# Gate sums as contraction rows of the score matmul, one constant causal tile, and unsplit float32 scores for every second head of batch 0

## The chip, the cores and the metric

The kernel runs on one core of one Trainium2 chip. The metric is the device time of one execution in microseconds (us), as the median of several runs. TensorE (PE; its weight loads are PEld) does the matmuls, VectorE (DVE), ScalarE (ACT) and GpSimd (POOL) the elementwise work, and SyncE (SP) issues all DMAs from one queue, in order.

## The reference, cut to what matters

Three stages follow each other on a batch of 4, 8 heads, 576 positions and a head dimension of 64: causal attention with a forget gate, a SwiGLU layer (512 to 1536 to 512), and a SiLU layer (512 to 2048 to 512), the latter two on all 2304 tokens.

```python
scores = scale * np.matmul(q, k.transpose(0, 1, 3, 2))         # scale = 1/8
cum = np.cumsum(np.maximum(s, 0.0), axis=-1)
bias = -(cum[:, :, :, None] - cum[:, :, None, :])
scores = np.where(causal, -1000000000.0, scores + np.minimum(bias, 0.0))
attn = softmax(scores); x = attn @ v                            # then heads side by side
x = (silu(x @ w_gate) * (x @ w_val)) @ w_out
out = silu(x @ w_in) @ w_out2
```

In a row of scores the term of the row's own position is a constant, which softmax removes; what stays is, per key position, the running sum `cum` of that head, and the causal mask.

## The kernel before, in words

**Matmul forms.** Most matmuls are of the type fp32r, which keeps fewer bits than float32, so a float32 operand is split into a high and a low part (hi = rounded copy, lo = operand minus hi). The scores of a head (`a_scores`, line 227) use two matmuls per tile. The 128 contraction rows hold the 64 rows of K rounded (`ks`, upper half) and the remainder of K (lower half); the other side is Q rounded, twice (`qh`), and the remainder of Q, twice (`ql`). `a_split` (line 197) makes these four pieces: a rounding copy of K on ACT (line 207), one of Q on DVE or ACT by the batch (208), the subtraction for K's lower half (210, on DVE in batch 0 and on POOL later), the subtraction for Q (212, on POOL in batch 0 and on DVE later). The attention output of batch 0 (`a_pv`, `WHOLE_P`) is computed from unsplit float32 operands; such a matmul stands in the trace as two instructions.

**Gate and mask.** `setup` (128) computes `cum` for all 32 heads on DVE. Each head's row must stand on all 128 partitions (`cumb`): for the first two heads by a matmul with a picked column of the identity and two ACT copies (lines 183 to 187), for the others by a DMA that repeats the row of 576 numbers 128 times (189, 288 KB). For every score tile POOL makes a masked copy of the part of `cumb` that holds the diagonal (line 235), and one DVE instruction adds scores and gate and takes the row's minimum of the negated sum (line 250). Where the masked part does not begin at the tile's left edge this takes two such instructions.

**After the scores.** ACT takes the exponential with its row sum (260), DVE makes the reciprocal (269, 270), POOL scales the row (117, called at 274), PE transposes it (292), ACT and DVE move the transposes out of PSUM, and PE multiplies by V (328).

**Staging.** A head is done in two halves: A holds the query tiles of 64, 128 and 128 rows, B two of 128. Each of the 64 half heads is a slot. Slot u emits the scores of unit u, the split of the next head and the loads of the head after it (with half A), the product with V of unit u-2 and the transposes of unit u-1 (`slot_pieces`, 548). The 18 first slots (all of batch 0) stand ahead of the feed-forward stream; the weights of its first two chunks are loaded and decoded from slot 8 on. After that, each chunk of the first layer carries two slots of the next batch between its steps. The weights come as 8 bytes per number on first use, are decoded by ACT and DVE (413 to 420), written back as float32 to DRAM (423) and read again in later batches; ACT, POOL and DVE split them (433, 434). The second layer follows with no attention left.

**What sets the order.** Instructions are emitted in the order of `body` (575), and a planner places them on each engine by emission order among those that its own timing has ready. On the chip each engine then runs its list in order. Pools limit how far ahead things go: two buffers of `qkr` (Q and K as loaded), `cumb`, `ks`, `qh`, `ql`, V; six of the score rows `e`, where `cum` and the setup's scratch tiles live at first.

Of the kernel before, what the change touches and what calls it, by code (L numbers as in the profile page):

```python
# [17 lines left out]
P = 128  # L18
# [49 lines left out]
def kernel(  # L68
# [98 lines left out]
    def a_load(b, h, halves):  # L167
        k1, v1, q0 = SPAN[halves]
        t = qkr_p.tile([P, 2, S], F32, tag="qkr", name="qkr")
        rows = (0,) if (b, h) in WHOLE_S else (0, D)  # L170
        if q0 == 0:
            src = qk[b, h, :, :, :k1].rearrange("t d s -> d t s")
            for lo in rows:
                nc.sync.dma_start(out=t[lo : lo + D, :, :k1], in_=src)
        else:
            for lo in rows:
                nc.sync.dma_start(out=t[lo : lo + D, 0, q0:k1], in_=qk[b, h, 0, :, q0:k1])
                nc.sync.dma_start(out=t[lo : lo + D, 1, :k1], in_=qk[b, h, 1, :, :k1])
        c = cum_p.tile([P, S], F32, tag="cumb", name="cumb")
        hh = b * H + h  # L180
        if hh < 2:
            for n0, n in ((0, min(k1, 320)), (320, k1 - 320)):
                if n > 0:
                    ps = ps_a.tile([P, 512], F32, tag="a", name="pcb")
                    pick = ident[: B * H, hh : hh + 1].to_broadcast([B * H, P])
                    nc.tensor.matmul(out=ps[:, :n], lhsT=pick, rhs=cum[:, n0 : n0 + n], start=True, stop=True)
                    nc.scalar.activation(out=c[:, n0 : n0 + n], in_=ps[:, :n], func=AF.Copy)
        else:
# [5 lines left out]
        st[b, h, halves] = (t, c, xa, xb)  # L194
        loads.append(last)

    def a_split(b, h, halves):
        k1, v1, q0 = SPAN[halves]
        t, c, xa, xb = st.pop((b, h, halves))
        if (b, h) in WHOLE_S:  # L200
            ks, qs = t[:D, 1], (t[:D, 0],)
        else:
            ks = qks_p.tile([P, S], F32R, tag="ks", name="ks")
            qh = qks_p.tile([P, S], F32R, tag="qh", name="qh")
            ql = qks_p.tile([P, S], F32R, tag="ql", name="ql")
            qs = (qh, ql)
# [3 lines left out]
            eng.tensor_tensor(out=ks[D:P, :k1], in0=t[D:P, 1, :k1], in1=ks[D:P, :k1].bitcast(F32), op=ALU.subtract)  # L210
            eng = nc.gpsimd if b in POOL_QL else nc.vector
            eng.tensor_tensor(out=ql[:, q0:k1], in0=t[:, 0, q0:k1], in1=qh[:, q0:k1].bitcast(F32), op=ALU.subtract)
        if (b, h) not in WHOLE_P:
            va_s = first_v[(b * H + h) % 3]
            vb_s = v_p.tile([P, 4, 2, D], F32R, tag="vsb", name="vsb")
            copy(VHI[b], va_s[:D, 0, :], xa)
            copy(VHI[b], vb_s[:, :v1, 0, :], xb[:, :v1])
            nc.vector.tensor_tensor(out=va_s[:D, 1, :], in0=xa, in1=va_s[:D, 0, :].bitcast(F32), op=ALU.subtract)
            eng = nc.gpsimd if b in POOL_V else nc.vector
            eng.tensor_tensor(  # L220
                out=vb_s[:, :v1, 1, :], in0=xb[:, :v1], in1=vb_s[:, :v1, 0, :].bitcast(F32), op=ALU.subtract
            )
            xa, xb = va_s.rearrange("p t d -> p (t d)"), vb_s.rearrange("p j t d -> p j (t d)")
        for half in halves:
            st[b, h, half, "in"] = (ks, qs, c, xa, xb)

    def a_scores(b, h, half, i):
        ks, qs, c, _, _ = st[b, h, half, "in"]
        q0, r = TILES[i]
        wd = q0 + r  # L230
        e = e_p.tile([P, S], F32, tag="e", name="e")

        g0 = 0 if wd <= 320 else 320
        nc.gpsimd.affine_select(
            out=e[:r, g0:wd], in_=c[:r, g0:wd], pattern=[[-1, wd - g0]], compare_op=ALU.is_ge,
            fill=-8.0 * QMASK, base=q0 - g0, channel_multiplier=1,
        )
        m = None
        for c0, n in ((0, wd),) if wd <= 512 else ((0, g0), (g0, wd - g0)):
            ps = ps_a.tile([P, 512], F32, tag="a", name="psc")  # L240
            for part, q in enumerate(qs):
                nc.tensor.matmul(
                    out=ps[:, :n], lhsT=q[:, q0 : q0 + P], rhs=ks[:, c0 : c0 + n],
                    start=(part == 0), stop=(part == len(qs) - 1),
                )
            for g, end, gate in ((c0, min(g0, c0 + n), c), (max(g0, c0), c0 + n, e)):
                if g >= end:
                    continue
                m2 = sm_p.tile([P, 1], F32, tag="m", name="m")
                nc.vector.tensor_tensor_reduce(  # L250
                    out=e[:r, g:end], in0=ps[:r, g - c0 : end - c0], in1=gate[:r, g:end], scale=-0.125,
                    scalar=3.0e38 if m is None else m[:r], op0=ALU.add, op1=ALU.min, accum_out=m2[:r],
                )
                m = m2
# [424 lines left out]
```

## Time and profile before

| | us |
|---|---|
| median of 3 runs | 1103.63 |
| lowest, highest | 1102.15, 1104.18 |
| profiled execution, first to last instruction (its span) | 1102.4 |
| PE busy in it | 1073.2 |
| DVE, ACT, POOL busy | 705.1, 587.2, 532.7 |

The profiled execution shows no time of its own beside its span; its span lies between the lowest and the highest of the timed runs. The page's PE share is an upper reading, since matmuls are pipelined and their ends are modelled; how far apart matmuls start is the better one. The profile's rows are given further down.

### The profile page before, as it was taken

How to read it: one execution, taken by the hardware profiler on the slowest of the kernel's cores; microseconds unless marked ns; L12 is line 12 of the kernel's file. 1: busy time of each engine (PE TensorE's matmuls, PEld its weight loads, DVE VectorE, ACT ScalarE, POOL GpSimd, SP SyncE). 2: the span in 40 equal slices, each digit the busy share in tenths (PEclk: the TensorE clock that was granted, in tenths of full speed). 3: DMA queues.
4: the chain of work that ended last, by engine and by line, in shares of the span. 5: the costliest groups of instructions: out<-in, count | busy, mean ns of one | idle time of the engine just before them, and what ended most of it. 6: DMA issues, size and time to landing. Idle time of an engine off the chain costs nothing. (4 is left out here: it accounts for less than half of the span.)

```text
span 1102.4 us, 19356 instructions
## 1 busy us (share of the span) xinstructions
PE 1073.2 (97%) x6760; PEld 994.2 (90%) x6760; DVE 705.1 (64%) x1625; ACT 587.2 (53%) x1294; POOL 532.7 (48%) x611
## 2 busy tenths in 40 slices
PE   7979899999999999999999999999999999999998
PEld 4647899999999999999999999888989898888887
DVE  6877788897778886868765346715364645644333
ACT  4887788875766564666645434655243433422221
POOL 7666677675666664757434453232323222332221
PEclk9988999999999999999999999999999999999999
DMA  5587487785353534533144223711010101000012
GB/s 135 137 242 239 157 216 239 210 250 174 86 143 90 140 95 140 149 83 101 39 154 147 77 86 123 226 41 59 20 58 20 58 20 58 20 1 1 1 61 111
DMA packets 53728, 121.39 MB, mean 110 GB/s; under 512 B 8256, under 2 KB 21568, under 8 KB 53632
## 3 DMA queue, kind: packets, MB, share of 16 engines
q1 hardware_dynamic: 53632, 120.17, 36.8%
q8 instruction: 53, 0.87, 0.3%
q14 instruction: 43, 0.35, 0.1%
HBM read 101.20 MB, written 18.95 MB: 109 GB/s over the span
## 5 line engine op out<-in xcount | busy, mean ns | idle before, releaser
L460 POOL TENSOR_TENSOR h<-u,h 128x288 fp32r<-128x288 f32 (+2 forms) x176 | 193.2, 1099 | 349.5 <-ACT h L113 344.7
L445 PE MATMUL po<-h,wh 128*128 128x288 f32 (+2 forms) x704 | 232.8, 332 | 2.1 <-ACT h L113 1.2
L446 PE MATMUL po<-h,wh 128*128 128x288 f32 (+2 forms) x704 | 232.9, 331 | 0.1
L445 PE MATMUL pgv<-xt,wh 128*128 128x288 f32 x768 | 230.9, 301 | 1.4 <-DVE u L458 0.8
L447 PE MATMUL po<-h,wl 128*128 128x288 f32 (+2 forms) x704 | 232.0, 330 | 0.0
L446 PE MATMUL pgv<-xt,wh 128*128 128x288 f32 x768 | 228.8, 298 | 1.5 <-DVE xt L349 1.5
L447 PE MATMUL pgv<-xt,wl 128*128 128x288 f32 x768 | 228.6, 298 | 0.0
L434 POOL TENSOR_TENSOR wl<-wraw,wh 128x1024 fp32r<-128x1024 f32 x53 | 129.2, 2437 | 113.8 <-ACT wh L113 101.5
L113 ACT ACTIVATE h<-u 128x288 fp32r<-128x288 f32 (+2 forms) x176 | 89.4, 508 | 118.0 <-DVE u L458 66.4
L445 PEld LDWEIGHTS pgv<-xt,wh 128*128 128x128 f32 x768 | 144.9, 189 | 3.0 <-DVE u L458 1.1
L446 PEld LDWEIGHTS pgv<-xt,wh 128*128 128x128 f32 x768 | 145.2, 189 | 2.0 <-DVE xt L349 1.8
L447 PEld LDWEIGHTS pgv<-xt,wl 128*128 128x128 f32 x768 | 145.1, 189 | 0.3
L445 PEld LDWEIGHTS po<-h,wh 128*128 128x128 f32 x704 | 132.0, 188 | 10.2 <-ACT h L113 1.8
L456 DVE SCALAR_TENSOR_TENSOR u<-th,pu 128x464 f32<-128x464 f32 (+1 forms) x80 | 50.7, 633 | 137.9 <-ACT th L454 137.9
L447 PEld LDWEIGHTS po<-h,wl 128*128 128x128 f32 x704 | 132.2, 188 | 7.0
L446 PEld LDWEIGHTS po<-h,wh 128*128 128x128 f32 x704 | 132.2, 188 | 6.9 <-POOL h L460 0.5
L540 DVE SCALAR_TENSOR_TENSOR acc<-po,acc 128x464 f32<-128x464 f32 (+1 forms) x140 | 88.5, 636 | 62.6 <-PE po L447 61.9
L454 ACT ACTIVATE th<-pu 128x464 f32<-128x464 f32 (+1 forms) x80 | 44.1, 552 | 152.2 <-PE pu L447 152.2
L113 ACT ACTIVATE wh<-wraw 128x1024 fp32r<-128x1024 f32 x88 | 92.2, 1056 | 52.0 <-PE po L446 27.1
L446 PE MATMUL pu<-x,wh 128*128 128x464 f32 (+1 forms) x320 | 118.9, 371 | 0.0
L445 PE MATMUL pu<-x,wh 128*128 128x464 f32 (+1 forms) x320 | 118.6, 371 | 0.0
L447 PE MATMUL pu<-x,wl 128*128 128x464 f32 (+1 forms) x320 | 118.5, 370 | 0.0
(87 smaller groups left out, 2012.9 us busy)
## 6 DMA issues: line engine op xcount, KB each, us to landing
wraw<-w SPq DMA_DIRECT2D x54, 512.0 KB, 4.8
r<-in_w_dram SPq DMA_DIRECT2D x52, 512.0 KB, 5.0
qkr<-in_qk_dram SPq DMA_DIRECT2D x64, 288.0 KB, 5.1
w<-wraw SPq DMA_DIRECT2D x18, 512.0 KB, 4.4
cumb<-cum_d SPq DMA_DIRECT2D x30, 288.0 KB, 4.1
r<-in_w_dram SPq DMA_DIRECT2D x32, 256.0 KB, 3.1
x_d<-acc SPq DMA_DIRECT2D x32, 144.0 KB, 3.8
vrb<-in_vb_dram SPq DMA_DIRECT2D x32, 128.0 KB, 4.6
```

Of the source, the lines that this page charges most:

```text
L113: nc.scalar.activation(out=out, in_=in_, func=AF.Copy, scale=scale)
L434: engines[eng].tensor_tensor(out=wl, in0=t, in1=wh.bitcast(F32), op=ALU.subtract)
L445: nc.tensor.matmul(out=ps[:, :n], lhsT=a, rhs=xh, start=(k == 0), stop=False)
L446: nc.tensor.matmul(out=ps[:, :n], lhsT=a, rhs=xl, start=False, stop=False)
L447: nc.tensor.matmul(out=ps[:, :n], lhsT=c, rhs=xh, start=False, stop=(k == last))
L454: nc.scalar.activation(out=th[:, :n], in_=pg[:, :n], func=AF.Tanh, scale=0.5)
L456: nc.vector.scalar_tensor_tensor(out=u, in0=th[:, :n], scalar=1.0, in1=pg[:, :n], op0=ALU.add, op1=ALU.mult)
L460: engines[LO[ph]].tensor_tensor(out=lo, in0=u, in1=hi.bitcast(F32), op=ALU.subtract)
L540: nc.vector.scalar_tensor_tensor(out=a, in0=ps[:, :n], scalar=0.5, in1=a, op0=ALU.mult, op1=ALU.add)
```

## The change

Per head, the gate is no longer added on DVE from a tile of 128 equal rows. It enters the score matmul as contraction rows: against rows of ones on Q's side stand the high and the low part of the head's `cum` row on K's side. Split heads (28 of 32) now use the pairs (`qa`,`ka`) and (`qb`,`kb`): `ka` is K rounded, twice; `qa` is Q rounded in the upper half and Q's remainder in the lower; `kb` holds the remainder of K in 64 rows, two gate rows, and zeros; `qb` holds Q rounded again, two rows of ones, and zeros. `kb` and `qb` are two fixed pairs of tiles whose zeros and ones are written once on POOL. The two gate rows come by a DMA from a DRAM table `cum_d` that now holds high part, low part and whole of every row. The mask is one constant tile `gate_c`, of which every score tile reads a shifted window, so each score tile takes one DVE instruction per PSUM bank. Heads 0, 2, 4 and 6 of batch 0 are not split: their scores are one float32 matmul per bank over 65 rows (64 of Q and K, one of ones and `cum`), straight from the loaded tile.

```diff
-WHOLE_S = []
+WHOLE_S = [(0, h) for h in (0, 2, 4, 6)]
+QUP = "gagg"
-    cum_p = pool("cum", 2, scope=attention, side="right")
+    row_p = pool("row", 1, scope=attention, side="right")
-    cum_d = dram.tile([B * H, S], F32, name="cum_d")
+    chl = [e_p.tile([B * H, S], F32, tag="e", name="chl") for _ in range(2)]
+    cum_d = dram.tile([B * H, 3, S], F32, name="cum_d")
+    gate_c = row_p.tile([P, 448 + P], F32, name="gate")
 def setup():
-        nc.sync.dma_start(out=cum_d, in_=cum)
+        nc.scalar.activation(out=chl[0].bitcast(F32R), in_=cum, func=AF.Copy)
+        nc.vector.tensor_tensor(out=chl[1].bitcast(F32R), in0=cum, in1=chl[0], op=ALU.subtract)
 def zeros():
         nc.gpsimd.memset(z[D:P], 0.0)
+        for n in range(2):
+            kb = row_p.tile([P, S], F32R, tag=f"kb{n}", name="kb")
+            qb = row_p.tile([P, S], F32R, tag=f"qb{n}", name="qb")
+            copy("g", kb[D:P], z[D:P])
+            copy("g", qb[D:P], z[D:P])
+            nc.gpsimd.tensor_scalar(out=qb[D : D + 2], in0=z[D : D + 2], scalar1=1.0, ...)
+            kq_b.append((kb, qb))
+        nc.gpsimd.memset(gate_c, 0.0)
+        nc.gpsimd.affine_select(out=gate_c[:, 448:], ..., fill=-8.0 * QMASK, base=0, channel_multiplier=1)
 def a_load(b, h, halves):
-        rows = (0,) if (b, h) in WHOLE_S else (0, D)
-        ...
-        c = cum_p.tile([P, S], F32, tag="cumb", name="cumb")
-        if hh < 2:
-            ...                     (a matmul with a picked identity column, two ACT copies)
-        else:
-            nc.sync.dma_start(out=c[:, :k1], in_=cum_d[hh : hh + 1, :k1].to_broadcast([P, k1]))
+        for lo in (0,) if whole else (0, D):
+            nc.sync.dma_start(out=t[lo : lo + D], in_=src)
+        if whole:
+            nc.gpsimd.memset(t[D : D + 1, 0], 1.0)
+            nc.sync.dma_start(out=t[D : D + 1, 1], in_=cum[hh : hh + 1] if hh == 0 else cum_d[hh : hh + 1, 2])
 def a_split(b, h, halves):
-            copy(KHI[b], ks[:, :k1], t[:, 1, :k1])
-            copy(QHI[b], qh[:, q0:k1], t[:, 0, q0:k1])
-            eng.tensor_tensor(out=ks[D:P, :k1], in0=t[D:P, 1, :k1], in1=ks[D:P, :k1]..., op=ALU.subtract)
-            eng.tensor_tensor(out=ql[:, q0:k1], in0=t[:, 0, q0:k1], in1=qh[:, q0:k1]..., op=ALU.subtract)
+            nc.sync.dma_start(out=kb[D : D + 2].bitcast(F32), in_=cum_d[hh, :2])
+            copy(KHI[b], ka, t[:, 1])
+            copy(QHI[b], qa, t[:, 0])
+            copy(QUP[b], qb[:D], t[:D, 0])
+            eng.tensor_tensor(out=kb[:D], in0=t[:D, 1], in1=ka[:D].bitcast(F32), op=ALU.subtract)
+            eng.tensor_tensor(out=qa[D:P], in0=t[D:P, 0], in1=qa[D:P].bitcast(F32), op=ALU.subtract)
+            parts = ((qa, ka), (qb, kb))     # unsplit: parts = ((t[: D + 1, 0], t[: D + 1, 1]),)
 def a_scores(b, h, half, i):
-        nc.gpsimd.affine_select(out=e[:r, g0:wd], in_=c[:r, g0:wd], ..., fill=-8.0 * QMASK, ...)
...
-            for g, end, gate in ((c0, min(g0, c0 + n), c), (max(g0, c0), c0 + n, e)):
-                nc.vector.tensor_tensor_reduce(out=e[:r, g:end], in0=ps[...], in1=gate[:r, g:end], ...)
+            g0 = 448 - q0 + c0
+            nc.vector.tensor_tensor_reduce(out=e[:r, c0 : c0 + n], in0=ps[:r, :n], in1=gate_c[:r, g0 : g0 + n], ...)
 def body():
         a_load(*spans[0])
+        for i, x in enumerate((*chl, cum)):
+            nc.sync.dma_start(out=cum_d[:, i], in_=x)
```

## Rows read from the trace of the kernel before

**Rows 1.** The profile's page: the span, and busy us (share) xinstructions of each engine.
```profile
span 1102.4 us, 19356 instructions
...
PE 1073.2 (97%) x6760; PEld 994.2 (90%) x6760; DVE 705.1 (64%) x1625; ACT 587.2 (53%) x1294; POOL 532.7 (48%) x611
```

**Rows 2.** Four stretches: length, busy us per engine, granted clock, DMA share, GB/s.
```profile
28.30:44.90 16.60, 15.89 (x89) 10.24 (x88) 13.23 (x48) 13.35 (x38) 11.59 (x23) 1.00 0.53 137
60.00:90.00 30.00, 24.06 (x107) 14.54 (x106) 21.07 (x64) 25.72 (x64) 19.94 (x32) 0.83 0.93 272
90.00:140.00 50.00, 45.52 (x313) 42.73 (x312) 41.30 (x110) 37.48 (x87) 31.02 (x44) 0.93 0.62 192
200.00:700.00 500.00, 497.81 (x3780) 491.31 (x3779) 356.66 (x883) 294.18 (x678) 282.40 (x317) 1.00 0.44 129
```

**Rows 3.** Timeline of PE within one head of batch 0: start, duration, instruction.
```profile
32.03 0.45 PE L242 MATMUL psc<-ks,qh 128*128 128x448 f32 x1
...
33.36 0.64 PE L328 MATMUL pv<-ph,vra 64*64 64x256 f32 x2
33.93 1.73 PE L328 MATMUL pv<-ph,vrb 128*64 128x256 f32 x8
35.59 0.91 PE L292 MATMUL ptr<-ident,e 64*64 64x64 f32 x6
36.25 0.28 PE L242 MATMUL psc<-ks,qh 128*128 128x64 f32 x1
```

**Rows 4.** Groups by line and shape, whole span: count, busy us, mean ns, idle before.
```profile
L250 DVE CUSTOM_DVE_ANT_0 e<-psc,cumb 128x320 f32<-128x320 f32 x64 | 31.0, 484 | 3.5 <-PE psc L242 3.1 <-DMA qkr<-in_qk_dram 0.3
L113 ACT ACTIVATE ks<-qkr 128x576 fp32r<-128x576 f32 x32 | 21.5, 672 | 10.1 <-DMA qkr<-in_qk_dram 6.4 <-PE psc L242 3.7
L115 DVE TENSOR_SCALAR qh<-qkr 128x576 fp32r<-128x576 f32 x24 | 14.1, 588 | 1.9 <-DMA qkr<-in_qk_dram 1.6 <-PE psc L242 0.2
L212 POOL TENSOR_TENSOR ql<-qkr,qh 128x576 fp32r<-128x576 f32 x8 | 12.3, 1539 | 7.1 <-PE pv L328 3.6 <-DVE qh L115 3.4
L210 DVE TENSOR_TENSOR ks<-qkr,ks 64x576 fp32r<-64x576 f32 x8 | 11.4, 1429 | 0.5 <-ACT ks L113 0.2
L250 DVE CUSTOM_DVE_ANT_0 e<-psc,e,m 128x128 f32<-128x128 f32 x32 | 11.0, 343 | 0.9
```

**Rows 5.** Groups by line, shapes together, whole span: the masked copies on POOL.
```profile
L234 POOL TENSOR_SCALAR_AFFINE_SELECT e<-cumb 64x64 f32<-64x64 f32 (+4 forms) x160 | 66.2, 436 | 19.5 <-PE ptr L292 18.9
```

**Rows 6.** Timeline of POOL at the start of the kernel.
```profile
1.35 0.57 POOL L153 MEMSET z<- 64x576 f32 x1
2.02 0.29 POOL L117 TENSOR_SCALAR vsa<-z 64x128 fp32r<-64x128 f32 x1
2.29 0.46 POOL L117 TENSOR_SCALAR ph<-z 64x320 fp32r<-64x320 f32 x1
...
5.51 0.50 POOL L117 TENSOR_SCALAR vsa<-z 64x128 fp32r<-64x128 f32 x1
```

**Rows 7.** Timeline of PE at the start of the kernel.
```profile
10.10 0.74 PE L242 MATMUL psc<-ks,qh 128*128 128x64 f32 x2
...
11.79 0.57 PE L242 MATMUL psc<-ks,qh 128*128 128x448 f32 x1
12.16 0.57 PE L242 MATMUL psc<-ks,ql 128*128 128x448 f32 x1
...
15.58 0.63 PE L292 MATMUL ptr<-ident,e 128*64 128x128 f32 x2 [1.47 <-POOL e L117]
```

**Rows 8.** DMA issues from 60 to 90 us: count, KB each, median us to landing.
```profile
cumb<-cum_d SPq DMA_DIRECT2D x2, 288.0 KB, 6.1
```

**Rows 9.** Timeline of all engines around 76.6 us.
```profile
76.60 2.36 POOL L434 TENSOR_TENSOR wl<-wraw,wh 128x1024 fp32r<-128x1024 f32 x1
...
76.75 2.24 DVE L269 TENSOR_SCALAR l<-l 128x2 f32<-128x2 f32 x1 [0.30 <-ACT e L260]
```

**Rows 10.** Waits of the SP queue, 60 to 140 us: total us, times, longest.
```profile
SPq L423 <- DVE wraw L418: 20.9, 3, 13.2
```

More of the change, by code (lines that the diff above doesn't have):

```diff
@@ L122 @@
     cum = e_p.tile([B * H, S], F32, tag="e", name="cum")
-    cum_d = dram.tile([B * H, S], F32, name="cum_d")
+    chl = [e_p.tile([B * H, S], F32, tag="e", name="chl") for _ in range(2)]
+    cum_d = dram.tile([B * H, 3, S], F32, name="cum_d")
+    gate_c = row_p.tile([P, 448 + P], F32, name="gate")
+    kq_b = []
     w32 = dram.tile([NGV + NO1, P, CW], F32, name="w32")
@@ L153, in zeros @@
         nc.gpsimd.memset(z[D:P], 0.0)
+        for n in range(2):
[3 more added lines that the diff above has]
+            copy("g", qb[D:P], z[D:P])
+            nc.gpsimd.tensor_scalar(
+                out=qb[D : D + 2], in0=z[D : D + 2], scalar1=1.0, scalar2=1.0, op0=ALU.add, op1=ALU.mult
+            )
+            kq_b.append((kb, qb))
+        nc.gpsimd.memset(gate_c, 0.0)
+        nc.gpsimd.affine_select(
+            out=gate_c[:, 448:], in_=gate_c[:, 448:], pattern=[[-1, P]], compare_op=ALU.is_ge,
+            fill=-8.0 * QMASK, base=0, channel_multiplier=1,
+        )
         for n in range(3):
@@ L169, in a_load @@
         t = qkr_p.tile([P, 2, S], F32, tag="qkr", name="qkr")
-        rows = (0,) if (b, h) in WHOLE_S else (0, D)
[L171 to L174, printed above, removed]
-        else:
-            for lo in rows:
-                nc.sync.dma_start(out=t[lo : lo + D, 0, q0:k1], in_=qk[b, h, 0, :, q0:k1])
-                nc.sync.dma_start(out=t[lo : lo + D, 1, :k1], in_=qk[b, h, 1, :, :k1])
-        c = cum_p.tile([P, S], F32, tag="cumb", name="cumb")
-        hh = b * H + h
-        if hh < 2:
[L182 to L188, printed above, removed]
-            nc.sync.dma_start(out=c[:, :k1], in_=cum_d[hh : hh + 1, :k1].to_broadcast([P, k1]))
+        src = qk[b, h].rearrange("t d s -> d t s")
+        whole = (b, h) in WHOLE_S
+        for lo in (0,) if whole else (0, D):
+            nc.sync.dma_start(out=t[lo : lo + D], in_=src)
+        if whole:
+            hh = b * H + h
+            nc.gpsimd.memset(t[D : D + 1, 0], 1.0)
+            nc.sync.dma_start(out=t[D : D + 1, 1], in_=cum[hh : hh + 1] if hh == 0 else cum_d[hh : hh + 1, 2])
         xa = v_p.tile([64, D], F32, tag="vra", name="vra")
@@ L193, in a_load @@
         last = nc.sync.dma_start(out=xb[:, :v1], in_=vb[b, h, :, :v1])
-        st[b, h, halves] = (t, c, xa, xb)
+        st[b, h, halves] = (t, xa, xb)
         loads.append(last)
@@ L198, in a_split @@
         k1, v1, q0 = SPAN[halves]
-        t, c, xa, xb = st.pop((b, h, halves))
+        t, xa, xb = st.pop((b, h, halves))
         if (b, h) in WHOLE_S:
-            ks, qs = t[:D, 1], (t[:D, 0],)
+            parts = ((t[: D + 1, 0], t[: D + 1, 1]),)
         else:
[L203 to L206, printed above, removed]
-            copy(KHI[b], ks[:, :k1], t[:, 1, :k1])
-            copy(QHI[b], qh[:, q0:k1], t[:, 0, q0:k1])
+            hh = b * H + h
+            kb, qb = kq_b[hh % 2]
+            nc.sync.dma_start(out=kb[D : D + 2].bitcast(F32), in_=cum_d[hh, :2])
+            ka = qks_p.tile([P, S], F32R, tag="ka", name="ka")
+            qa = qks_p.tile([P, S], F32R, tag="qa", name="qa")
+            copy(KHI[b], ka, t[:, 1])
+            copy(QHI[b], qa, t[:, 0])
+            copy(QUP[b], qb[:D], t[:D, 0])
             eng = nc.gpsimd if b in POOL_KS else nc.vector
-            eng.tensor_tensor(out=ks[D:P, :k1], in0=t[D:P, 1, :k1], in1=ks[D:P, :k1].bitcast(F32), op=ALU.subtract)
+            eng.tensor_tensor(out=kb[:D], in0=t[:D, 1], in1=ka[:D].bitcast(F32), op=ALU.subtract)
             eng = nc.gpsimd if b in POOL_QL else nc.vector
-            eng.tensor_tensor(out=ql[:, q0:k1], in0=t[:, 0, q0:k1], in1=qh[:, q0:k1].bitcast(F32), op=ALU.subtract)
+            eng.tensor_tensor(out=qa[D:P], in0=t[D:P, 0], in1=qa[D:P].bitcast(F32), op=ALU.subtract)
+            parts = ((qa, ka), (qb, kb))
         if (b, h) not in WHOLE_P:
@@ L224, in a_split @@
         for half in halves:
-            st[b, h, half, "in"] = (ks, qs, c, xa, xb)
+            st[b, h, half, "in"] = (parts, xa, xb)
     def a_scores(b, h, half, i):
-        ks, qs, c, _, _ = st[b, h, half, "in"]
+        parts = st[b, h, half, "in"][0]
         q0, r = TILES[i]
@@ L231, in a_scores @@
         e = e_p.tile([P, S], F32, tag="e", name="e")
[L233 to L237, printed above, removed]
         m = None
-        for c0, n in ((0, wd),) if wd <= 512 else ((0, g0), (g0, wd - g0)):
+        for c0, n in ((0, wd),) if wd <= 512 else ((0, 320), (320, wd - 320)):
             ps = ps_a.tile([P, 512], F32, tag="a", name="psc")
-            for part, q in enumerate(qs):
+            for part, (qq, kk) in enumerate(parts):
                 nc.tensor.matmul(
-                    out=ps[:, :n], lhsT=q[:, q0 : q0 + P], rhs=ks[:, c0 : c0 + n],
-                    start=(part == 0), stop=(part == len(qs) - 1),
-                )
-            for g, end, gate in ((c0, min(g0, c0 + n), c), (max(g0, c0), c0 + n, e)):
[L247 to L254, printed above, removed]
+                    out=ps[:, :n], lhsT=qq[:, q0 : q0 + P], rhs=kk[:, c0 : c0 + n],
+                    start=(part == 0), stop=(part == len(parts) - 1),
+                )
+            m2 = sm_p.tile([P, 1], F32, tag="m", name="m")
+            g0 = 448 - q0 + c0
+            nc.vector.tensor_tensor_reduce(
+                out=e[:r, c0 : c0 + n], in0=ps[:r, :n], in1=gate_c[:r, g0 : g0 + n], scale=-0.125,
+                scalar=3.0e38 if m is None else m[:r], op0=ALU.add, op1=ALU.min, accum_out=m2[:r],
+            )
+            m = m2
         if i in (0, 1, 3):
@@ L318, in a_pv @@
         tiles, base, n = HALF[half]
-        _, _, _, wa, wb = st.pop((b, h, half, "in"))
+        _, wa, wb = st.pop((b, h, half, "in"))
         whole = (b, h) in WHOLE_P
```

## The prediction

> **What bounds the kernel now.** I read the page first. PE is busy in 97% of the span, the others in 48 to 64% [rows 1]: over the whole kernel TensorE is the limit, so only work of PE, or a stall of PE, is worth time. The table of stretches says where such stalls are. From 200 to 700 us PE is busy 497.8 of 500 us at a granted clock of 1.00; what happens there on DVE, POOL and DMA is covered. Between 60 and 90 us it is busy 24.1 of 30 us with the clock at 0.83 (part of the stretch at 1.2 GHz, the rest at 2.4) while the DMA engines are at 0.93 and ACT at 25.7 of 30; between 90 and 140 us, 45.5 of 50 at 0.93 [rows 2]. All of batch 0, where the unsplit heads are, stands ahead of the feed-forward stream, so the change must earn or lose its time in the first 140 us or so.
>
> In batch 0 two heads take 16.6 us (28.3 to 44.9), 8.3 us each, and PE reads as busy 15.9 of them, which sounds full, but DVE and ACT are at 13.2 and 13.4 and POOL at 11.6 [rows 2]. The timeline gives PE's own pace, by the distance between starts: 8 instructions of V's product, 6 of 256 and 2 of 128 columns, take 33.93 to 35.59, so 1.66 us for 1792 columns, 0.93 ns each; 6 transposes take 0.66 us (35.59 to 36.25); the six score matmuls of half B take 32.03 to 33.36, 1.33 us for 2 times 1024 columns [rows 3]. Per head: V's product, 1856 columns twice, 3.4 us; 15 transposes, 1.65; scores, 1600 columns twice at half B's 0.65 ns, 2.1. That is 7.2 of 8.3 us: about 1.1 us per head is slack, spread over short waits on the other engines. No engine is alone the limit there.
>
> The Trainium skill, page "Perfetto Trace Analysis", section "Identifying the Most-Contended Engine", says that matmul busy time misleads and that the share of weight loading is the better measure. That share is 10.2 of 16.6 us here [rows 2]. By it PE would have 3.2 us free per head, by the busy row 0.35; the distances between starts say 1.1, and I keep them.
>
> **The change part by part.** *Unsplit scores on PE.* A head's 1600 score columns, in float32 two instructions each at the pace of V's product, cost 3200 x 0.93 = 3.0 us. Before: 2.1 us by half B, or 1.4 us if the fp32r matmuls ran at the 0.21 us that 448 columns would need at 2.4 GHz. So +0.9 to +1.6 us per unsplit head. The trace has no matmul of 65 rows; the nearest, V's first of 64 rows, steps 0.57 us for twice 256 columns (33.36 to 33.93) against 0.47 at the other pace [rows 3]: if this lack of cover for the weights holds for 12 instructions, +0.6 more. I take +1.0, since the pieces of before also carry such gaps; ends 0.9 and 2.2.
>
> *What the other engines shed there.* An unsplit head loses the rounding copies of K on ACT (0.67) and of Q on DVE (0.59), the subtractions on DVE (1.43) and POOL (1.54) [rows 4]. Every head loses five masked copies on POOL, 66.2/32 = 2.07 us [rows 5], and one of two DVE additions of the 448-wide tile: 484 and 343 ns become one that by the slope between them (0.73 ns per column) costs 578, so -0.25 us [rows 4]. A split head gains a copy of 64x576: in batch 0, 2 and 3 on POOL, 0.69 us by extending 0.29 us for 128 and 0.46 for 320 columns [rows 6]; in batch 1 on ACT, 0.67 us by the row of K's copy.
>
> *Heads 2 to 5.* Unsplit: PE 7.2 + 1.0 = 8.2 us, just the present 8.3, while DVE falls by 2.3, ACT by 0.7 and POOL by 3.0 (with 0.57 for the ones row, priced as the memset [rows 6]). Split: PE unchanged, DVE -0.25, POOL -1.4. I take -0.1 for the former and -0.3 for the latter, -0.8 for two pairs. Ends: -3 (all waits of PE on DVE and POOL go) and +4.4 (PE's 2.2 fully added twice).
>
> *Start.* POOL now also writes four zero halves and two ones (6 x 0.69), the constant tile (0.57 and a select of 0.44), and the ones row of head 0 (0.57) ahead of the first score: its list ended at 6.01 us [rows 6], so it ends near 11.7, where the first score began at 10.10 [rows 7]; +1.5. Head 0 runs at the lower clock (448 columns step 0.37 us, 1.2 GHz): PE fell idle 1.47 us before 15.58, so at 14.1, after these scores and one transpose of about 0.3 us [rows 7], which leaves 3.7 us for the scores; in float32, twice the 3.0, 5.9 us; +2.2. The idle 1.47 us behind takes in most of the former, and POOL's gap-filling work there (a subtraction of 1.5 us and five masked copies) is gone; the broadcast matmuls that stood before 10.10 were in nobody's way. Net +1.0; ends -2 (the dense float32 scores bring the clock up earlier) and +3.7.
>
> *60 to 90 us, where the first weights come in.* Two gate broadcasts of 288 KB leave this stretch [rows 8]; at its 272 GB/s [rows 2] that is 0.59 MB, 2.2 us. The two rows of gate that replace them are 4.6 KB. The weight decode and the tail of batch 0 wait for these DMAs. With DVE's 2.3 us for head 6 in the same stretch I take -2.5; ends -5 and 0 (another wait closes the gap).
>
> *90 to 200 us.* Each head of batch 1 sheds 288 KB and 2.07 us of POOL, and puts 0.67 us more on ACT, which is at 37.5 of 50. PE's holes here are 4.5 us and the low clock [rows 2]. I take -1.5, most of it DMA; ends -4 and +3 (five heads' ACT copies late).
>
> *200 us on.* The scores are still two fp32r matmuls, so PE's work is the same; 0, ends -1 and +1.
>
> Sum: +1.0 - 0.8 - 2.5 - 1.5 = -3.8 us. It is made against the profiled execution, 1102.4 us with nothing outside its span; the runs' median lies 1.2 us above it, and the change is taken off that: 1103.6 - 3.8 = 1099.8 us.
>
> **The rivals.** *Slower: PE is the limit of batch 0.* Place: heads 0, 2, 4, 6. Price: the start at its upper end, +3.7, and three heads at 2.2 less the slack of 1.1, +3.3; the bytes still give 2.2 back: +4.8, 1108.4 us. It decides once the 65-row weights are not covered. For it: PE's busy 15.9 of 16.6 us; against it: the 1.1 us of slack by starts.
>
> *Slower: the gate rows come late.* Each split head's second matmul now waits for a small DMA in SP's one queue, and SP stands still for up to 13.2 us, 20.9 in all from 60 to 140 us, behind the write-back of decoded weights [rows 10]. The rows are issued a head ahead, 8 to 18 us, so one or two heads could be held for about 4 us each: with the rest of the sum 1099.8 + 6 = 1106.
>
> *No change: the relief is off the path.* The front waits for weights, whose order on SP is not changed; the cost on PE eats the 2.2 us of bytes: 1103.
>
> *More: DVE is held by POOL.* A DVE instruction on 128x2 numbers lasted 2.24 us while POOL's subtraction of 2.36 us ran, both ending together [rows 9]. If the masked copies hold DVE in this way, each head from 28 to 140 us, some eleven of them, loses up to 2.07 us more of waiting; a quarter of it on the path gives -5.7: 1094. The Trainium skill, page "SBUF — State Buffer", section "Who interferes with whom", has this as a rule (one shared port pair, held for the whole instruction), and the trace agrees with 2.24 us; but the same rule charges the new POOL copies of the split heads.
>
> *It doesn't do what it says:* excluded as a cause of its own; the masked copies and broadcasts can't stay, only come back as waits.
>
> **How the numbers follow.** About 0.2%, 2.2 us, can be told from no change. Forecast 0.48 (1095.5 to 1101.4), more 0.07, no change 0.20, PE-bound 0.16, late gate rows 0.09. Faster 0.55, same 0.20, slower 0.25. The range 1093 to 1108 leaves out the upper rival's half and little below.
>
> **What would show it.** Right: the first score near 11 to 12 us; 12 float32 score instructions of an unsplit head in about 3.0 us; two heads of batch 0 in 16.2 instead of 16.6 us; no 288 KB gate DMAs; the first `pgv` matmul 2 to 4 us earlier than now, and PE's busy time from 200 to 700 us as now. Wrong: unsplit heads of over 9 us, a wait of the scores on the gate rows' DMA, or a front as long as now.

## The result: 1.0% slower, and the profile after

The kernel after takes 1114.8 us (median of 4 runs, 1114.36 to 1118.23), the kernel before beside it 1103.91: a ratio of 1.0103 [1.0076, 1.0130]. The forecast was 1099.8 us, with 1108 as its upper end. The page after, against [rows 1]:

```profile
span 1116.4 us, 18949 instructions
...
PE 1078.6 (97%) x6752; PEld 995.6 (89%) x6752; DVE 696.2 (62%) x1554; ACT 588.1 (53%) x1295; POOL 485.4 (43%) x479
...
DMA packets 49076, 111.63 MB, mean 100 GB/s; under 512 B 7835, under 2 KB 21147, under 8 KB 48982
```

The other engines were relieved: POOL lost 47.3 us of busy time, DVE 8.9, and 9.8 of 121.4 MB of transfers are gone. None of it became time. The medians lie 10.9 us apart, the two profiles 14.0, since the profiled execution after is the longest of its four (1118.23). To see where these 14.0 us arise, both are cut at the same events: the first score of head 2, the first score of head 6, the first chunk's first `pgv` matmul, and the start of the second pass over the weights (from batch 1's feed-forward on). Before, then after; the columns are the stretch, its length, busy us (instructions) of PE, PEld, DVE, ACT and POOL, granted clock, DMA share, GB/s:

```profile
0.00:28.30 28.30, 20.36 (x69) 14.27 (x69) 19.00 (x53) 13.27 (x35) 19.95 (x38) 1.00 0.55 134
28.30:61.20 32.90, 31.73 (x175) 20.49 (x174) 26.55 (x96) 26.20 (x74) 23.37 (x45) 1.00 0.50 133
61.20:90.20 29.00, 23.06 (x101) 13.72 (x99) 20.07 (x65) 25.17 (x61) 18.98 (x31) 0.82 0.95 275
90.20:265.60 175.40, 168.28 (x1241) 162.22 (x1241) 152.16 (x404) 133.69 (x311) 122.06 (x154) 0.98 0.73 214
265.60:1102.40 836.80, 829.76 (x5183) 783.51 (x5182) 487.35 (x1010) 388.86 (x816) 348.34 (x345) 1.00 0.27 81
```

```profile
0.00:32.10 32.10, 18.61 (x61) 12.17 (x62) 13.98 (x47) 12.25 (x32) 19.01 (x37) 1.00 0.31 76
32.10:67.50 35.40, 33.68 (x174) 20.87 (x173) 20.69 (x84) 24.06 (x70) 15.07 (x25) 1.00 0.27 68
67.50:99.30 31.80, 25.24 (x110) 14.58 (x108) 20.03 (x65) 27.16 (x67) 15.28 (x18) 0.87 0.88 258
99.30:280.50 181.20, 172.04 (x1232) 164.80 (x1231) 151.78 (x379) 136.90 (x314) 105.56 (x112) 0.96 0.64 192
280.50:1116.40 835.90, 829.04 (x5184) 783.23 (x5182) 489.71 (x980) 387.72 (x816) 330.45 (x287) 1.00 0.25 76
```

The differences are +3.8 (start), +2.5 (heads 2 to 5), +2.8, +5.8 and -0.9 us. Everything is decided before the second pass; the last 836 us are as they were. The two middle stretches are best read together, as +8.6: the first of them holds 110 instructions of PE where it held 101, so work has moved across the cut between them.

**Heads 2 to 5.** PE's timeline of head 4 after, from its first score to head 5's (start, duration, instruction):

```profile
49.96 1.56 PE L245 MATMUL psc<-qkr 65*128 65x64 f32 x6
51.46 0.75 PE L329 MATMUL pv<-ph,vra 64*64 64x320 f32 x2
52.14 0.86 PE L329 MATMUL pv<-ph,vrb 128*64 128x256 f32 x4
52.93 1.17 PE L293 MATMUL ptr<-ident,e 128*64 128x128 f32 x9
53.94 1.89 PE L245 MATMUL psc<-qkr 65*128 65x448 f32 x6
55.76 0.64 PE L329 MATMUL pv<-ph,vra 64*64 64x256 f32 x2
56.33 1.73 PE L329 MATMUL pv<-ph,vrb 128*64 128x256 f32 x8
57.99 0.91 PE L293 MATMUL ptr<-ident,e 64*64 64x64 f32 x6
58.66 0.28 PE L245 MATMUL psc<-ka,qa 128*128 128x64 f32 x1
```

Each row begins where the one before lets it: PE stands back to back for 8.70 us, 3.32 of them the scores (49.96 to 51.46, 53.94 to 55.76). The same head before shows no stop either:

```profile
44.92 0.28 PE L242 MATMUL psc<-ks,qh 128*128 128x64 f32 x1
...
45.91 0.75 PE L328 MATMUL pv<-ph,vra 64*64 64x320 f32 x2
...
52.53 0.28 PE L242 MATMUL psc<-ks,qh 128*128 128x64 f32 x1
```

From 44.92 to head 5's first score at 52.53 are 7.61 us, with scores of 0.99 (44.92 to 45.91) and of 1.33 in half B, as in [rows 3]: 2.32 in all. Heads 2 to 5 took 7.93, 8.67, 7.61 and 8.67 us before and take 9.03, 8.79, 8.69 and 8.85 after: +1.1 in each even head, +0.1 and +0.2 in the odd ones. So an even head had almost nothing free; the pair's stops were in the odd head.

**Start.** POOL's timeline after:

```profile
2.75 0.84 POOL L157 MEMSET z<- 64x576 f32 x1
7.05 0.66 POOL L118 TENSOR_SCALAR qb<-qkr 64x576 fp32r<-64x576 f32 x1 [3.46 <-DMA qkr<-in_qk_dram]
7.80 0.67 POOL L118 TENSOR_SCALAR kb<-z 64x576 fp32r<-64x576 f32 x1
...
13.52 1.43 POOL L220 TENSOR_TENSOR qa<-qkr,qa 64x576 fp32r<-64x576 f32 x1
14.90 0.66 POOL L163 TENSOR_SCALAR qb<-z 2x576 fp32r<-2x576 f32 x1
15.66 0.31 POOL L118 TENSOR_SCALAR e<-e,rl 64x64 f32<-64x64 f32 x1
```

The copy of head 1's Q stands in POOL's list ahead of the zeros and waits 3.46 us for its load; the zeros follow, then head 1's subtraction and a row of ones, and only then, at 15.66, the scaling of head 0's first row tile. PE waits for it, and again behind ACT, where a piece of a later head stands waiting for its load ahead of the copies of `ph`:

```profile
16.02 0.31 PE L293 MATMUL ptr<-ident,e 64*64 64x64 f32 x1 [1.62 <-POOL e L118]
...
21.24 0.68 ACT L114 ACTIVATE ka<-qkr 128x576 fp32r<-128x576 f32 x1 [2.20 <-DMA qkr<-in_qk_dram]
...
22.30 1.32 PE L329 MATMUL pv<-ph,vra 64*64 64x320 f32 x2 [2.40 <-ACT ph L114]
```

The scores themselves began at 8.52, earlier than the 10.10 of [rows 7]. That head 0 ran at the lower clock shows in the pace of its scores alone (1.84 ns per column and instruction against 1.04 in head 4); the granted clock reads 1.00 for the whole start.

### The profile page after: what moved, and what is told of

Same layout as the page of the kernel before. It is cut to its first block, busy times and chain, and to the rows that moved or that the text cites. A ratio compares the mean times of both kernels' runs of the same rounds, so it can differ in the third digit from the quotient of the medians.

```text
span 1116.4 us, 18949 instructions
## 1 busy us (share of the span) xinstructions
PE 1078.6 (97%) x6752; PEld 995.6 (89%) x6752; DVE 696.2 (62%) x1554; ACT 588.1 (53%) x1295; POOL 485.4 (43%) x479
## 5 line engine op out<-in xcount | busy, mean ns | idle before, releaser
L461 POOL TENSOR_TENSOR h<-u,h 128x288 fp32r<-128x288 f32 (+2 forms) x176 | 190.0, 1081 | 347.7 <-ACT h L114 340.4
L118 POOL TENSOR_SCALAR e<-e,rl 64x64 f32<-64x64 f32 (+4 forms) x160 | 85.8, 547 | 91.7 <-DVE rl L271 48.5
```

What stands on the lines that cost most here:

```text
L118: nc.gpsimd.tensor_scalar(out=out, in0=in_, scalar1=scale, scalar2=1.0, op0=ALU.mult, op1=ALU.mult)
L461: engines[LO[ph]].tensor_tensor(out=lo, in0=u, in1=hi.bitcast(F32), op=ALU.subtract)
```

## The experiments

Ratios are to the kernel before, run on the same chip. In us, from the profiles: S is the start up to head 2, H heads 2 to 5, R head 6 to the second pass. They come from one execution of each kernel, and executions of one kernel lie up to 8.6 us apart (e17: 1116.00 to 1124.58, the profiled one being the longest), so a small difference in R says little.

| run | ratio [95%] | S | H | R |
|---|---|---|---|---|
| before | 1 | 28.3 | 32.9 | 204.4 |
| after | 1.0103 [1.0076, 1.0130] | 32.1 | 35.4 | 213.0 |
| e1_split_all | 1.0197 [1.0178, 1.0215] | 36.0 | 32.9 | 221.4 |
| e2_unsplit_alone | 1.0144 [1.0123, 1.0164] | 28.1 | 45.1 | 208.3 |
| e3_alternate | 1.0091 [1.0070, 1.0111] | 31.9 | 36.1 | 208.6 |
| e4_zeros_off_pool | 1.0041 [1.0026, 1.0056] | 26.5 | 35.0 | 209.0 |
| e5_copy_on_pool | 1.0128 [1.0092, 1.0164] | 26.5 | 35.3 | 221.8 |
| e6_split_zeros | 1.0206 [1.0181, 1.0231] | 32.3 | 33.2 | 222.8 |
| e7_one_pass | 1.0114 [1.0091, 1.0138] | 28.3 | 33.7 | 217.2 |
| e8_head0_only | 1.0087 [1.0059, 1.0115] | 28.8 | 32.6 | 217.2 |
| e9_late_split | 1.0090 [1.0061, 1.0120] | 27.0 | 35.2 | 215.2 |
| e10_late_only | 1.0145 [1.0119, 1.0171] | 31.9 | 35.1 | 214.0 |
| e11_late_head0 | 1.0072 [1.0047, 1.0098] | 28.6 | 32.5 | 209.3 |
| e12_before_late | 1.0103 [1.0067, 1.0139] | 27.7 | 32.9 | 218.5 |
| e13_alternate_zeros | 1.0109 [1.0086, 1.0131] | 26.0 | 37.6 | 212.5 |
| e14_zeros_head0 | 1.0097 [1.0073, 1.0122] | 29.5 | 32.5 | 217.5 |
| e15_no_pair_writes | 1.0167 [1.0137, 1.0197] | 32.3 | 35.3 | 222.0 |
| e16_no_gate_dma | 1.0117 [1.0086, 1.0148] | 30.9 | 35.3 | 209.2 |
| e17_before_split_end | 1.0118 [1.0087, 1.0150] | 29.3 | 32.9 | 220.6 |
| e18_split_end | 1.0112 [1.0085, 1.0140] | 26.9 | 35.3 | 211.9 |

### Unsplit heads

e1_split_all: after, with
```
-WHOLE_S = [(0, h) for h in (0, 2, 4, 6)]
+WHOLE_S = []
```


> The changed kernel with no unsplit head: all 32 heads are split and use the gate rows. Theory A (the unsplit float32 scores make PE the limit of heads 0, 2, 4 and 6, about 1 us each, and 1 to 2 us more in head 0 at the lower clock): some 4 us faster than the changed kernel, near 1110. Theory B (the fixed gate-row tiles: in batch 0 only odd heads are split and all use the same pair, so SP stands 12 us behind head 1's scores): now the pairs alternate from head to head, this wait is gone, 1106 to 1109, though DVE and POOL get their splitting back. Theory C (POOL's zeros and ones hold up the start): no difference to the start, heads 0 and 1 late as in the changed kernel.

H is 32.9 us, that of before, although DVE, ACT and POOL are relieved: the relief of split heads is off PE's path. The start is worse (36.0), as head 0 then needs all its pieces, and the whole takes 1127 us where theories A and B had 1106 to 1110.

e2_unsplit_alone: the kernel before with `+WHOLE_S = [(0, h) for h in (0, 2, 4, 6)]`.


> The kernel before, with the gate still added on DVE, but heads 0, 2, 4 and 6 unsplit (64 rows, one float32 matmul per bank). Theory A: slower than before by 3 to 5 us, near 1108, with the unsplit heads 1 us longer each. Theories B and C (gate rows, zeros): the cause is elsewhere, so with DVE and POOL relieved 1099 to 1104.

H is 45.1, which no theory had. By the waits, unsplit heads read the loaded tile until their last score, so one of its two buffers comes free late, and SP stands at the next load (13.6 us over batch 0). But the change has this hold too (13.0 us behind PE `pv`, below) with an H of 35.4, so it is not shown to be the whole cause.

e7_one_pass: e4 (below), and the unsplit scores from the upper 16 bits of each number, in one instruction of PE instead of two:
```
-            parts = ((t[: D + 1, 0], t[: D + 1, 1]),)
+            tb = t.bitcast(mybir.dt.bfloat16).rearrange("p t (s w) -> p t s w", w=2)[:, :, :, 1]
+            parts = ((tb[: D + 1, 0], tb[: D + 1, 1]),)
```


> The changed kernel with zeros by ACT and ones by DVE, and the four unsplit heads' scores taken from the upper 16 bits of Q and K (one pass instead of four: this leaves out the lower half of every number, so the scores are coarser). Only PE's work differs. Theory A (PE is the limit of the unsplit heads): heads 2, 4 and 6 fall from 8.7 us to 7.5 or less, 4 to 6 us faster than with float32 scores, 0.999 of before or less. Rival (held buffers, DMA and in-order waits set the 8.7 us): they stay over 8.2 us and the time stays near 1.004.

Even heads fall from 8.7 to 7.3 us, and odd ones take 9.5 instead of 8.8: the second instruction is on the path, and about half of what it frees is lost in the odd head. The run as a whole is 0.7% slower than e4, with R at 217.2 instead of 209.0, so theory A has its heads but not its time. Over all runs H is 32.5 to 33.2 us with these heads split and 35.0 to 36.1 with them unsplit, e2, e7 and e13 apart.

### Start

e4_zeros_off_pool: after, with
```
-            copy("g", kb[D:P], z[D:P])
-            copy("g", qb[D:P], z[D:P])
-            nc.gpsimd.tensor_scalar(out=qb[D : D + 2], ...)
+            copy("a", kb[D:P], z[D:P])
+            copy("a", qb[D:P], z[D:P])
+            nc.vector.tensor_scalar(out=qb[D : D + 2], ...)
```


> The changed kernel, but the zeros of the gate-row tiles are written by ACT and the ones by DVE. Theory C: POOL scales head 0's rows 2 to 3 us earlier, head 1's scores come near 15.5 instead of 17.6 us and head 2's near 29 instead of 32, 3 us faster: near 1112. Theories A and B: PE in head 0 and SP's wait remain, within 1 us of 1115.

S falls by 5.6 us to 26.5, below that of before. POOL still waits for the load, but what is behind it is shorter, and head 0's first scaling begins 2 us earlier:

```profile
7.39 0.67 POOL L118 TENSOR_SCALAR qb<-qkr 64x576 fp32r<-64x576 f32 x1 [3.82 <-DMA qkr<-in_qk_dram]
...
11.03 1.61 POOL L220 TENSOR_TENSOR qa<-qkr,qa 64x576 fp32r<-64x576 f32 x1
13.68 0.32 POOL L118 TENSOR_SCALAR e<-e,rl 64x64 f32<-64x64 f32 x1 [1.04 <-DVE l L270]
```

e6_split_zeros: e4 with `WHOLE_S = []`.


> All heads split, gate rows for all, zeros by ACT and ones by DVE. Theory A (each unsplit head costs PE about 1 us): heads 2 to 6 take 16.4 us a pair as before, not 17.5, and the start is relieved of POOL's zeros, so from 1.0197 (all split, zeros on POOL) down to 1.003 to 1.008. Theory B (the split heads' wait for gate rows and for the fixed pairs is what costs): still 1.012 or more, with head 1 split late at the start and heads of over 8.3 us.

S rises to 32.3, 5.8 us above e4's. Head 0 takes 12.6 us instead of 6.8, since its scores now need their pieces. Head 0 alone unsplit (e14, below) wins back 2.8 of the 5.8 (S 29.5): head 1 then takes 13.9 us, and 11.1 in e4, where head 2 is unsplit too.

### The gate rows' DMA in SP's queue

e3_alternate: after, with the split heads of batch 0 using both pairs in turn, where the odd heads all used one:
```
-            kb, qb = kq_b[hh % 2]
+            kb, qb = kq_b[(hh // 2 if b == 0 else hh) % 2]
```


> The changed kernel, but the split heads of batch 0 (1, 3, 5, 7) alternate between the two pairs of gate-row tiles. Theory B: the wait of SP on head 1's scores (12.1 us, to 29.1) goes, the loads behind it come earlier, 2 to 4 us faster than the changed kernel: 1111 to 1113. Theories A and C: within 1 us of the changed kernel, 1114 to 1116.

The waits of SP up to 60 us, after and then e3 (line and releaser: us in total, times, longest):

```profile
SPq L211 <- PE psc L245: 18.1, 2, 12.1
SPq L191 <- PE pv L329: 13.0, 2, 6.7
```
```profile
SPq L191 <- PE pv L329: 12.8, 2, 6.4
SPq L191 <- DMA qkr<-in_qk_dram: 7.2, 2, 4.3
```

The stand of 12.1 us at the gate rows is gone and the time is the same within the intervals; R fell by 4.4 us, H rose by 0.7 and the rest of the kernel by 2.4.

e13_alternate_zeros: e3's edit in e4.


> Zeros off POOL and alternating pairs in batch 0 together. Theory (start and the stretch from head 6 to the first chunk have separate causes, POOL's zeros and the odd heads' one pair): start 26.5, heads 2 to 6 in 35, 27.7 to the first chunk instead of 31.6, so the first chunk at 89.2 us, 1 us ahead of the kernel before; with 177.4 for the weight stretch the time is about 1106. Rival (the gain ahead is given back, since weights come no earlier): first chunk at 92 to 93 and 1110.

The two gains don't add: S is 26.0, but H 37.6 and R 212.5. The first chunk came at 95.8 us, later than either theory had it.

### From the first weights to the second pass

e5_copy_on_pool: e4 with `QUP = "gggg"` (the copy of Q for batch 1 on POOL). e8_head0_only: that, and `WHOLE_S = [(0, 0)]`. e14_zeros_head0: e4 with `WHOLE_S = [(0, 0)]`.


> The changed kernel with zeros by ACT and ones by DVE (as in the run before this), and the copy of Q for the second pair on POOL in batch 1 too, not on ACT. Theory D (in the first pass of the weights ACT's eight extra copies of 0.67 us stand in line with the weight decode): the stretch from the first chunk to the second pass of chunk 0 shrinks by 3 to 5 us, and the time falls from 1.0041 of before to about 1.000. Rival E (that stretch is longer because the split waits for the single pair of gate-row tiles, or because the planned order no longer fits): no change, 1.003 to 1.005 of before.

> As the first of these (zeros by ACT, ones by DVE, copies on POOL), but only head 0 unsplit, which lets the first scores begin without a split and without gate rows. Theory A: three heads less with 1 us extra on PE, 2 to 3 us faster than with four, 0.997 to 1.000 of before. Theory B: head 1 to 7 all use gate rows now, 1.004 or more.

> Zeros off POOL, only head 0 unsplit, so heads 2, 4 and 6 are split again and the seven split heads alternate between the pairs. Theory (an unsplit head costs about 1.1 us behind the start, and helps in the start): start about 28, heads 2 to 6 in 32.8, 30 to the first chunk, weight stretch 177 to 180: 1105 to 1108. Rival (unsplit heads give more to POOL and DVE than they cost PE): 1110 or more, with a longer weight stretch.

Taking batch 1's copies off ACT did not shorten R: with them on POOL it is 12.8 us longer than in e4, which neither theory had. POOL's waits in e5's weight stretch have a new leader, which was 4.7 us after and does not appear in e4:

```profile
POOL qb L118 <- PE psc L245: 25.2, 8, 6.3
POOL wl L435 <- ACT wh L114: 20.3, 11, 4.6
```

That suggested the fixed pairs as the cause: what is written into them waits, in an engine's order, for scores of two heads earlier, with the weights' pieces behind. e14 has e8's heads with the copy back on ACT, and R is no shorter.

e9_late_split: e4; e10_late_only: after; e11_late_head0: e4 with `WHOLE_S = [(0, 0)]`; e12_before_late: before; each with
```
-            if half == sp[0]:
-                n = spans.index((b, h, sp))
+            n = spans.index((b, h, sp))
+            late = n + 1 < len(spans) and spans[n + 1][0] > 0
+            if half == (sp[-1] if late else sp[0]):
```


> The run with the zeros off POOL, with one more edit: from batch 1 on, a head's split and the loads behind it are emitted after the scores of the head before's half B instead of its half A, so that the pieces that are written into the two fixed pairs of tiles no longer stand in POOL's and ACT's lists ahead of scores which they wait for. Theory F (the pieces of the next head stand in order in front of the weights' pieces and wait for PE's scores): the waits of POOL and ACT on PE's scores between the first weight chunk and the second pass fall under 3 us, that stretch takes 174 to 176 us instead of 177.4, and the time goes from 1110 to about 1107. Rival G (the stretch is long because each new order of the instructions is less lucky than the one before): no connection, the stretch anywhere from 177 to 186 us. Rival T (a late split makes the scores wait for their own pieces): waits of PE on kb or qb, 1112 or more.

> The changed kernel with the late split of batches 1 to 3 alone. Theory F: the waits on PE's scores of ACT's ka (7.1 us), POOL's qb (4.7) and wl (5.5) in the weight stretch shrink to under 3 us each, the stretch goes from 181.2 to 176 us, the time from 1114.8 to about 1110; the stretches before it (heads 2 to 6, 35.4 us, and start, 32.1) stay. Rival G: the stretch stays within 180 to 187 us. Rival T: PE waits for split pieces, 1117 or more.

> Zeros off POOL, late split, and only head 0 of batch 0 unsplit. The same with the early split (and batch 1's copy on POOL) had the weight stretch at 187.3 us. Theory F: 175 to 177 us there, a start of about 28, heads 2 to 6 in 32.6, 30 to the first weight chunk, so about 1104, level with the kernel before. Rival G: 180 to 187 us there and 1110 to 1116.

> Control: the kernel before with the late split alone. Its pieces lie in rotating pairs of buffers and POOL had no wait on the scores there. Theory F: nothing to win, within 0.3% of 1104 us, the weight stretch at 174 to 177 us. Rival G (any new order costs): the stretch rises by 5 us or more. Rival T: 1107 or more with PE waiting for ks, qh or ql.

The theory of the fixed pairs misses: R rose in e9 and e10, and POOL's waits on `qb` grew to 7.3 and 9.6 us. Only e11 has a short R, 8.2 us below e14's, and it too came out 9 us above its 1104. The control is what counts: the kernel before, with no fixed pair, lost 14.1 us in R by the same edit.

e15_no_pair_writes: after, without the DMA, copy and subtraction into the pairs:
```
+            if hh < 10:
                 nc.sync.dma_start(out=kb[D : D + 2].bitcast(F32), in_=cum_d[hh, :2])
...
+            if hh < 10:
                 copy(QUP[b], qb[:D], t[:D, 0])
...
+            if hh < 10:
                 eng.tensor_tensor(out=kb[:D], in0=t[:D, 1], ...)
```
e16_no_gate_dma: after, with `if b == 0:` before the DMA alone.


> The changed kernel without what is written into the two fixed pairs from the third head of batch 1 on: no gate rows' DMA, no copy of Q, no subtraction for K (the second matmul of those heads reads what the pairs hold; this part of the computation is left out). Theory F (these writes wait in order for PE's scores and hold weights' pieces): SP's waits at that DMA (39 us) and POOL's on qb (4.7) are gone, the weight stretch falls from 181.2 to 175 us or less, the time to 1108 or less. Theory O (the order of the instructions as such, with the clock's dips behind short stops of PE): it stays at 178 to 187 us though DMAs, copies and subtractions are gone.

> The changed kernel without the gate rows' DMA from batch 1 on (the gate of these heads is left out). If SP's standing at that DMA (39 us between 80 and 280 us) holds the weights' loads back: the weight stretch falls by 3 us or more, and with e15 to the same level. If the copies and subtractions are what holds: 180 to 182, as now, and 1114 to 1116. Theory O: anywhere in 177 to 187 us.

Without these writes from the third head of batch 1 on, R is 222.0 us, 9 more than after; 4.8 of the 9 lie ahead of the first chunk, where the writes are still those of after, and behind it are 185.4 us against 181.2. So taking these writes out did not shorten R. That their waits cost nothing is not shown, since such an edit draws a new order too (next section), in which a gain of some us can hide. Without the DMA alone it is 209.2, and the ratio is that of after within the intervals.

### Order alone

e17_before_split_end: the kernel before; e18_split_end: e4; each with the next head's split and the loads emitted at the end of slot A:
```
-            if half == sp[0]:
-                n = spans.index((b, h, sp))
-                if n + 1 < len(spans):
-                    pcs.append(lambda x=spans[n + 1]: a_split(*x))
...
             pcs.append(lambda b=b, h=h, half=half: a_transpose(b, h, half))
+        if u < len(units) and half0 == sp0[0]:
+            n = spans.index((b0, h0, sp0))
+            if n + 1 < len(spans):
+                pcs.append(lambda x=spans[n + 1]: a_split(*x))
...
```


> The kernel before with the split of the next head and the loads of the one after it emitted at the end of slot A, behind the product with V and the transposes, instead of right behind the scores; no work changes. Theory O (in this stretch the order as such is worth some per cent, and the kernel before stands at the good end): head 6 to the second pass takes 209 to 220 us instead of 204.4 and the time is 1108 to 1118. Rival C (what the change itself adds makes the difference): 203 to 206 us there and 1102 to 1107.

> The same reordering in the run with the zeros off POOL (209.0 us from head 6 to the second pass, 1110 us). Theory O: anywhere from 204 to 220 us, more than 3 us away from 209.0. Rival C: within 2 us of 209.0 and 1108 to 1112.

e17 does the same instructions as before in R and needs 220.6 us for them instead of 204.4. The row of R, of before and then of e17:

```profile
61.20:265.60 204.40, 191.34 (x1341) 175.94 (x1340) 172.22 (x467) 158.85 (x371) 141.04 (x185) 0.96 0.76 223
```
```profile
62.20:282.80 220.60, 198.09 (x1341) 179.77 (x1340) 180.73 (x467) 160.89 (x371) 140.20 (x185) 0.95 0.71 207
```

The counts are equal on every engine. PE idles 22.5 us instead of 13.1, and its busy time grows by 6.8 us with the same instructions. None of PE's waits in R is for the pieces or loads that were moved; the longest, 6.1 us in five, are those of `pgv` for the decoded weights. Order alone is thus worth 16 us between these two executions, and by the ratios (1.0118 against 1.0103) about as much as the change lost. e18 moved R by 2.9 us, just short of what the theory of order asked for, and is 0.7% slower than e4.

## Why the prediction was wrong

**"The weight decode and the tail of batch 0 wait for these DMAs": the step that failed most.** By it the bytes, with DVE's relief, were to give -2.5 us at 60 to 90 us and -1.5 at 90 to 200; measured are +2.8 up to the first chunk and +5.8 behind it, and the first `pgv` matmul came 9.1 us later, not 2 to 4 earlier. The bytes went, and the DMA share fell from 0.95 to 0.88, but fewer bytes did not bring the first chunk forward. R after, against that of before (shown at e17):

```profile
67.50:280.50 213.00, 197.27 (x1339) 179.38 (x1338) 171.81 (x444) 164.06 (x380) 120.83 (x130) 0.94 0.68 202
```

PE idles 15.7 instead of 13.1 us and is busy 5.9 us longer. One place is head 6, the unsplit head beside the first weights. It takes 14.0 us (67.50 to 81.50), where it took 8.8 before (61.20 to 69.97):

```profile
67.50 1.57 PE L245 MATMUL psc<-qkr 65*128 65x64 f32 x6
...
69.92 0.68 ACT L114 ACTIVATE qb<-qkr 64x576 fp32r<-64x576 f32 x1 [1.24 <-DMA qkr<-in_qk_dram]
...
73.40 3.48 PE L245 MATMUL psc<-qkr 65*128 65x448 f32 x6 [1.75 <-ACT x L114]
...
81.50 0.28 PE L245 MATMUL psc<-ka,qa 128*128 128x64 f32 x1
```

ACT's copy `qb` for batch 1, which the change added, waits 1.24 us for its load; `ka`, `qa` and then `x` stand behind it, PE stops for 1.75 us, and from 73.7 on the granted clock is 0.50 for 6.8 us. Over all runs head 6 takes 8.8 to 9.3 us where it is split and 10.7 to 15.1 where it is not, 12.6 with the one-pass scores of e7 and 12.8 with that copy on POOL (e5, where ACT's `ka` waits for its load instead). So this loss goes with the unsplit head and is more than the price of its scores. From head 7 to the first chunk it is the other way round: 17.8 us against 20.3 before, where the clock fell for 3.4 us (from 73.5) and 6.8 (from 80.3). So how much of head 6's 5.2 us stays in the end is not shown.

A second stop lies further on: ACT, DVE and PE after, around 140 us:

```profile
137.73 1.24 ACT L414 ACTIVATE wraw<-r 128x512 f32<-128x512 f32 x2 [4.76 <-DMA w<-wraw]
138.86 0.61 ACT L415 ACTIVATE dk<-r 128x512 uint32<-128x512 uint32 x1
...
139.51 0.70 DVE L416 SCALAR_TENSOR_TENSOR dk<-wraw,dk 128x512 uint32<-128x512 uint32 x1 [4.32 <-ACT dk L415]
140.23 0.48 DVE L344 TENSOR_TENSOR x<-pv,xtmp 64x320 f32<-64x320 f32 x1
...
140.77 0.47 PE L245 MATMUL psc<-ka,qa 128*128 128x448 f32 x1 [1.79 <-DVE x L344]
143.18 0.64 PE L245 MATMUL psc<-ka,qa 128*128 128x320 f32 x1 [1.74 <-DVE pl L311]
```

A decode step stands in ACT's list and waits 4.76 us for the write-back of a buffer; DVE's next decode step waits for it, and `x`, which frees the PSUM bank that PE needs, stands behind. PE stops for 1.79 and 1.74 us, and from 142.0 on the granted clock is 0.50 (1.2 GHz) for 6.8 us, so that PE's busy time grows too:

```profile
142.00:148.80 6.80, 5.62 (x23) 5.53 (x24) 6.26 (x16) 5.26 (x11) 2.85 (x2) 0.50 0.49 154
```

The kernel before has the same chain once, ACT and then PE, with the clock at 0.50 for 3.4 us behind it:

```profile
131.01 1.22 ACT L413 ACTIVATE wraw<-r 128x512 f32<-128x512 f32 x2 [4.12 <-DMA w<-wraw]
...
135.35 0.74 PE L242 MATMUL psc<-ks,qh 128*128 128x448 f32 x1 [2.93 <-DVE x L343]
```

After has one more stop of PE at 224, 2.01 us behind DVE's decode (`wraw`), and again 6.8 us at the lower clock. Which steps stand behind such a wait is a matter of order, and the change gave the planner other work and so another order. That an order can cost this much is shown by e12 and e17, and that taking out the writes into the pairs does not help by e15. How after's 8.6 us in R divide between head 6 and order stays open: of 18 other kernels none came below 208.3 us there, and no run gave the changed kernel the order of before.

**"About 1.1 us per head is slack."** This failed in two ways. The average of a pair hid that the even head was back to back (7.61 us in head 4) and the odd one held the stops. And the working counted all scores at half B's pace, 2.1 us, where head 4 took 2.32 before. The unsplit scores took 3.32 (predicted 3.0), so the price of +1.0 was right, and with no slack to take it in all of it was on the path: the term -0.1 per unsplit head measured +1.1. Heads 2 to 5: +2.5 instead of -0.8; the term of -0.3 for a split head was zero by e1. (The lower price of 1.4 us, at 0.21 us per 448 columns, should read 1.5; nothing hangs on it.) The Trainium skill, page "Perfetto Trace Analysis", section "Identifying the Most-Contended Engine", would have freed PE still more by its share of weight loading. That share is 5.17 of 8.70 us in head 4 after; PE, back to back there, disagrees with that reading.

**"Start +1.0."** Measured +3.8, about its upper end of +3.7 but by another mechanism. Head 0's float32 scores took the 5.9 us that were worked out (8.52 to 14.4), and began early. What was late was POOL's list behind the waiting copy: the prediction put the zeros ahead of the first score, where they cost 1.5 us, and did not ask what else stands behind them. e4 takes the zeros and ones out of that list and wins 5.6 us.

**The rivals.** "PE is the limit of batch 0" had the right place and the right price for heads 2 and 4 (+1.1 each), but counted the bytes as won. "The gate rows come late" was true of SP (12.1 us at one DMA) and cost nothing measurable by e3 and e16. "DVE is held by POOL" became no time: in e1's heads 2 to 5 POOL is busy 20.2 instead of 23.4 us and DVE 22.2 instead of 26.6, its subtraction on 64x576 numbers taking 740 instead of 1588 ns (whether by POOL's relief was not tested), and they take 32.9 us as before. "From 200 to 700 us as now" held but for a few us, the stop at 224 above all: PE is busy 494.3 of 500 us at 0.99.

No run beats the kernel before; e4 comes nearest, at 1.0041 [1.0026, 1.0056].

## What to carry to other kernels

Slack is read where the engine's starts have gaps, instruction by instruction and per kind of iteration, not from an average over two kinds. Work added to an in-order engine is priced by what stands behind it, above all behind an instruction that waits for a load. Where a planner sets the order, any edit also draws a new order: a control that only reorders the old kernel says what that is worth (here 1.2%, about the size of the whole effect), and a range without it is too narrow.

## What the runs showed that was not expected

Taking work out made the kernel slower: e15 has fewer DMAs, copies and subtractions than after, and its ratio is 1.0167 [1.0137, 1.0197] against 1.0103 [1.0076, 1.0130]. And the 12 float32 score instructions of 65 rows pace at 1.04 ns per column and instruction (3.32 us for twice 1600), against the 0.93 of V's product; in head 0, at the pace of the lower clock, it was 1.84 (5.88 us).
